# Routing for the first expert taken apart: records in a tensor of their own, one-hot products 128 columns wide, other experts' tables and the last scatters behind the branch

## The chip, the cores and the metric

One core of one Trainium2 chip runs the whole program. The metric is device time in microseconds, from launch to the end of the last engine; the median of three runs of the kernel before is 544.47 us (544.14 to 545.3). Engines are named as in the profile: PE multiplies matrices (PEld loads its weights), DVE, ACT and POOL work on 128 partitions at a time, SP issues loads and stores.

## What is computed

B = 1, S = 2048 tokens, D = 512, F = 1792, E = 8 experts, float32. Layer A is a long causal convolution, gated, with a residual; layer B sends each token to the one expert with the highest logit.

```python
h = x + q_ln * y                 # y: short conv of k, times v, long conv over S, plus kv * ssm_D
xf = layernorm(h)
logits = xf @ w_gate
topk_idx = argsort(-logits)[:, :1]
gates = softmax(topk_val)        # one value: 1
for e in range(E):
    mask = topk_idx == e
    out += (gates * mask) * (silu(xf @ w1[e]) @ w2[e])
h2 = h + out
```

## The kernel before

The program has three stages, all with an order written out by hand for each engine (a manual schedule: an engine runs its instructions in program order and waits on semaphores).

**Convolution and logits (0 to 182 us).** A planner interleaves loads, transposes, products with Toeplitz windows and DVE and POOL work. At its end, for each 128-wide block c of D, `logits(c, p)` (L388) multiplies the transposed rows with the gate weights; `sum_logits` adds the result to `lacc`. `h_dram` holds one row of 516 numbers per token: 512 of h, then mean, 1/std, gate and a spare.

**Routing (182 to 198.6 us).** PE transposes `lacc` into `pl` (L618). DVE finds each token's expert as a one-hot `oh` (P x E x NJ: token p of column j, NJ = 16), and a scan `incl` of it along j. PE makes the counts of the experts (`pn`) and the rank of every token within its expert (`pr`, L644, L645). DVE then makes `key` (count and index, L652), the sorted order of the experts (`gt`, `sr`, `eqm`, `perm_i`), and each token's place `c_i` in a table of 8 experts x 4 tiles x 128 rows, of which 24 tiles are kept. The place splits into a tile `col_i` and a row `lo_f`. `ohhi` marks the tile, POOL multiplies it with the token's number (`vt`), and `ohlo` marks the row; sixteen products `ohlo` x `vt` (L687), one for each j, add up to the table `ptab` (128 rows x 24 tiles) of token numbers plus one. From it come `idxg` (rows to gather) and, on POOL, `idxs` and `half_i` (rows to scatter to, with a large number for empty places). Two gathers on POOL (L707) fetch the first two tiles of the first expert (the smallest one); SP loads its first two weight chunks `raw` (L715). `keep_warm` (L605) issues products that nobody reads.

**Branch and experts (198.6 us to the end).** `over`, `nover` and `wide_i` compare the sizes of the experts with a list of capacities; every engine loads `wide_i` and jumps (L948). This input takes the block `experts(SNUG)`, laid out right behind. In it the experts run smallest first of `ORDER`: `norm` and `turn_x` normalise and transpose the gathered rows (`xr`, then `xh` and `xl`, a high and a low part), ACT and DVE split each weight chunk into `whi` and `wlo`, `up` (L821) makes acc = three sets of products, ACT its silu `s`, DVE `hh`, POOL `hl`; `down` (L842, L845) goes back; `send` (L855 and L857) adds the residual into `o` and scatters `o` to `out_dram` on POOL. In an expert's `up`, from chunk 3 on, POOL issues the gathers of the next expert's rows (`hr`, L759), one each chunk. The last expert's last rows leave in two halves. Behind the block stands the program's end (L1119): a DRAIN on each engine, SP's walk over all semaphores, and a barrier.

Of the kernel before, what the change touches and what calls it, by code (L numbers as in the profile page):

```python
# [11 lines left out]
I32 = mybir.dt.int32  # L12
AF = mybir.ActivationFunctionType
# [11 lines left out]
RW = D + 4  # L25
# [106 lines left out]
def kernel(  # L132
# [8 lines left out]
    h_dram = dram.tile([S, RW], F32, name="h_dram")  # L141
# [23 lines left out]
    iota_b = keep.tile([P, P], F16, name="iota_b")  # L165
# [11 lines left out]

    conv = ExitStack()
# [253 lines left out]
    def casts():  # L432
# [3 lines left out]
        for a, n in ((iota_b, "iota"), (tri_b, "tri"), (one_b, "one"), (tile_b, "tile")):  # L436
            nc.gpsimd.tensor_copy(a, const(n))
# [5 lines left out]
    nc.gpsimd.memset(wgc, 0.0)  # L443
    nc.scalar.activation(mv1[:, 0, 0:1], lacc[:, 0:1], AF.Copy)
# [155 lines left out]

    conv.close()
# [3 lines left out]
    def keep_warm(n, width):  # L605
        for _ in range(n):
# [3 lines left out]
    bc = lambda a, n: a.unsqueeze(2).to_broadcast([P, NJ, n])  # L610
# [8 lines left out]
    keep_warm(5, 128)  # L619
# [7 lines left out]
    nc.vector.reciprocal(rec[:, :, 1], rec[:, :, 1])  # L627
# [16 lines left out]
    nc.tensor.matmul(pr, tri_b, oh, start=True, stop=False)  # L644
    nc.tensor.matmul(pr, one_b, incl, start=False, stop=True)  # L645
# [6 lines left out]
    nc.vector.scalar_tensor_tensor(key, pn, float(E), const("key"), op0=ALU.mult, op1=ALU.add)  # L652
# [3 lines left out]
    gt = small([E, E], "gt")  # L656
    nc.vector.tensor_tensor(gt, key.unsqueeze(1).to_broadcast([P, E, E]),
                            key.unsqueeze(2).to_broadcast([P, E, E]), op=ALU.is_gt)
    sr = small([E], "sr")
    nc.vector.tensor_reduce(sr, gt, axis=AX.X, op=ALU.add)  # L660
    eqm = small([E, E], "eqm", parts=1)
    eqe = small([E, E], "eqe", parts=1)
    nc.vector.tensor_tensor(eqm, sr[0:1].unsqueeze(1).to_broadcast([1, E, E]),
                            const("si")[0:1].rearrange("p (i e) -> p i e", e=E), op=ALU.is_equal)
    nc.gpsimd.tensor_tensor(eqe, eqm, const("ei")[0:1].rearrange("p (i e) -> p i e", e=E), op=ALU.mult)

    r2 = small([E, NJ], "r2")
    nc.vector.scalar_tensor_tensor(r2, sr.unsqueeze(2).to_broadcast([P, E, NJ]), 4096.0, pr,
                                   op0=ALU.mult, op1=ALU.add)
    nc.vector.tensor_tensor(r2, r2, oh, op=ALU.mult)  # L670
    with nc.allow_low_precision(reason="whole numbers under 8"):
        nc.vector.tensor_reduce(perm_i, eqe, axis=AX.X, op=ALU.add)
    with nc.allow_low_precision(reason="whole numbers under 32768"):
        nc.vector.tensor_reduce(c_i, by_j(r2), axis=AX.X, op=ALU.add)
    nc.vector.tensor_scalar(col_i, c_i, 7, None, op0=ALU.logical_shift_right)
    nc.vector.scalar_tensor_tensor(lo_f, col_i, -float(P), c_i, op0=ALU.mult, op1=ALU.add)

    ohhi = small([NJ, 24], "ohhi", F16)
    nc.vector.tensor_tensor(ohhi, tile_b.unsqueeze(1).to_broadcast([P, NJ, 24]), bc(col_i, 24),
                            op=ALU.is_equal)  # L680
    vt = small([NJ, 24], "vt", F16)
    nc.gpsimd.tensor_tensor(vt, ohhi, bc(tok_b, 24), op=ALU.mult)
    ohlo = ohlo_f.bitcast(F16).rearrange("p (j m) -> p j m", j=NJ)
    ptab = ps_t.tile([P, 24], F32, name="pt")
    for j in range(NJ):
        nc.vector.tensor_scalar(ohlo[:, j, :], iota_b, lo_f[:, j:j + 1], None, op0=ALU.is_equal)
        nc.tensor.matmul(ptab, ohlo[:, j, :], vt[:, j], start=j == 0, stop=j == NJ - 1)  # L687
    keep_warm(4, 432)
# [5 lines left out]
    nc.vector.tensor_scalar(idxg, ptab, -1.0, 0.0, op0=ALU.add, op1=ALU.max)  # L694
# [3 lines left out]
    tabs = small([24], "tabs")  # L698
    nc.scalar.activation(tabs, ptab, AF.Copy)


    first = ctx.enter_context(tc.tile_pool(name="first", bufs=1))
    rows0 = []
    for t in range(2):
        hr = first.tile([P, RW], F32, name=f"first{t}")
        col = 3 * ORDER[0] + t
        nc.gpsimd.indirect_dma_start(  # L707
            out=hr, out_offset=None, in_=h_dram[:, :],
            in_offset=bass.IndirectOffsetOnAxis(ap=idxg[:, col:col + 1], axis=0))
        rows0.append(hr)  # L710
# [19 lines left out]
    def experts(caps):  # L730
# [392 lines left out]
```

## Time and profile before

The profile is of one execution on the chip.

| | |
|---|---|
| median of 3 runs | 544.47 us |
| the profiled execution, its time | 544.39 us |
| its span, first to last instruction | 542.5 us |
| mean granted clock of PE | 0.991 |
| PE busy | 519.1 us (96%) |
| DVE busy | 405.6 us (75%) |
| ACT busy | 265.1 us (49%) |
| POOL busy | 260.7 us (48%) |

Groups and timeline rows read: start or busy time, engine, line, operation, tile written and tiles read (buffer numbers left out), sizes, count, and in brackets how long the engine had been idle and what ended that. Rows of one source line read: engine, operation, count, least, median and greatest duration in ns, and the start of the first and of the last. PE and its weight loads PEld are listed apart.

### The profile page before, as it was taken

How to read it: one execution, taken by the hardware profiler on the slowest of the kernel's cores; microseconds unless marked ns; L12 is line 12 of the kernel's file. 1: busy time of each engine (PE TensorE's matmuls, PEld its weight loads, DVE VectorE, ACT ScalarE, POOL GpSimd, SP SyncE). 2: the span in 40 equal slices, each digit the busy share in tenths (PEclk: the TensorE clock that was granted, in tenths of full speed). 3: DMA queues.
4: the chain of work that ended last, by engine and by line, in shares of the span. 5: the costliest groups of instructions: out<-in, count | busy, mean ns of one | idle time of the engine just before them, and what ended most of it. 6: DMA issues, size and time to landing. Idle time of an engine off the chain costs nothing. (4 is left out here: it accounts for less than half of the span.)

```text
span 542.5 us, 12152 instructions
## 1 busy us (share of the span) xinstructions
PE 519.1 (96%) x4812; PEld 451.9 (83%) x4812; DVE 405.6 (75%) x558; ACT 265.1 (49%) x410; POOL 260.7 (48%) x297
## 2 busy tenths in 40 slices
PE   9999989999998699999999999999999999999994
PEld 9867767767656469789999999999988988988973
DVE  3779899898997968859855784974884784785851
ACT  2697887544320346545435445545543644554520
POOL 0555659865641136618503921840760760851832
PEclk9999999999999989999999999999999999999998
DMA  8918786659661278674654665674676566576401
GB/s 285 380 55 261 236 276 195 179 153 287 187 170 43 60 263 320 218 256 166 199 182 140 204 199 166 189 259 141 206 219 233 180 210 231 194 219 205 155 2 41
DMA packets 42468, 105.26 MB, mean 194 GB/s; under 512 B 6480, under 2 KB 14800, under 8 KB 42018
## 3 DMA queue, kind: packets, MB, share of 16 engines
q1 hardware_dynamic: 39602, 95.89, 54.9%
q0 software_dynamic: 2800, 8.51, 4.9%
q8 instruction: 40, 0.66, 0.5%
q14 instruction: 26, 0.21, 0.1%
HBM read 95.96 MB, written 8.47 MB: 193 GB/s over the span
## 5 line engine op out<-in xcount | busy, mean ns | idle before, releaser
L826 POOL TENSOR_TENSOR hl<-s,hh 128x240 fp32r<-128x240 f32 (+5 forms) x112 | 114.4, 1035 | 162.2 <-DVE hh L825 161.7
L807 DVE TENSOR_TENSOR wlo<-raw,whi 128x1024 fp32r<-128x1024 f32 x112 | 160.5, 1443 | 38.8 <-ACT whi L806 35.2
L806 ACT ACTIVATE whi<-raw 128x1024 fp32r<-128x1024 f32 x112 | 114.6, 1051 | 3.5 <-DMA raw<-in_w_dram 3.5
L824 ACT ACTIVATE s<-acc 128x240 f32<-128x240 f32 (+5 forms) x112 | 43.1, 387 | 98.1 <-PE acc L821 63.4
L825 DVE CAST hh<-s 128x240 fp32r<-128x240 f32 (+5 forms) x112 | 55.0, 501 | 30.1 <-ACT s L824 29.9
L821 PE MATMUL acc<-xh,whi 128*128 128x240 f32 (+5 forms) x448 | 73.0, 285 | 0.1
L821 PE MATMUL acc<-xh,wlo 128*128 128x240 f32 (+5 forms) x448 | 72.0, 283 | 0.0
L821 PE MATMUL acc<-xl,whi 128*128 128x240 f32 (+5 forms) x448 | 71.9, 283 | 0.0
L821 PEld LDWEIGHTS acc<-xh,whi 128*128 128x128 f32 x448 | 61.7, 189 | 0.8 <-ACT xh L782 0.3
L821 PEld LDWEIGHTS acc<-xl,whi 128*128 128x128 f32 x448 | 61.6, 189 | 0.0
L821 PEld LDWEIGHTS acc<-xh,wlo 128*128 128x128 f32 x448 | 61.4, 189 | 0.0
L842 PE MATMUL acc<-whi,hh 128*128 128x512 f32 (+2 forms) x136 | 54.3, 399 | 0.0
L842 PE MATMUL acc<-whi,hl 128*128 128x512 f32 (+2 forms) x136 | 53.6, 394 | 0.0
L842 PE MATMUL acc<-wlo,hh 128*128 128x512 f32 (+2 forms) x136 | 53.5, 394 | 0.0
L265 POOL TENSOR_TENSOR acc<-acc,ac 128x512 f32<-128x512 f32 x26 | 33.1, 1280 | 37.1 <-ACT acc L253 19.2
L845 PE MATMUL acc<-hh,whi 128*128 128x304 f32 (+2 forms) x168 | 49.8, 296 | 0.0
L845 PE MATMUL acc<-hl,whi 128*128 128x304 f32 (+2 forms) x168 | 49.2, 293 | 0.0
L845 PE MATMUL acc<-hh,wlo 128*128 128x304 f32 (+2 forms) x168 | 49.1, 292 | 0.0
L296 ACT ACTIVATE st<-pa 128x512 f32<-128x512 f32 x64 | 37.3, 595 | 20.6 <-PE pa L293 20.3
L293 PEld LDWEIGHTS pa<-kv,tw 128*128 128x128 f32 x256 | 30.2, 191 | 12.2 <-ACT st L296 8.7
L293 PE MATMUL pa<-kv,tw 128*128 128x128 f32 x256 | 33.5, 282 | 2.2 <-ACT st L296 2.2
L782 ACT ACTIVATE xh<-pt 128x512 fp32r<-128x512 f32 (+5 forms) x18 | 9.6, 535 | 53.1 <-PE pt L781 53.1
(171 smaller groups left out, 878.2 us busy)
## 6 DMA issues: line engine op xcount, KB each, us to landing
raw<-in_w_dram SPq DMA_DIRECT2D x112, 512.0 KB
tv<-in_tab_v_dram SPq DMA_DIRECT2D x12, 512.0 KB
h<-in_q_dram SPq DMA_DIRECT2D x16, 256.0 KB
kt<-in_kt_dram SPq DMA_DIRECT2D x3, 1216.0 KB
v<-in_v_dram SPq DMA_DIRECT2D x12, 256.0 KB
kern<-in_ssm_dram SPq DMA_DIRECT2D x12, 256.0 KB
h<-in_x_dram SPq DMA_DIRECT2D x12, 256.0 KB
h_dram<-h SPq DMA_DIRECT2D x12, 256.0 KB
```

The lines of the kernel that those rows point to most:

```text
L265: nc.gpsimd.tensor_add(T[a, c, u], T[a, c, u], T[b, c, u])
L293: nc.tensor.matmul(p[:, :, j], tw[:, u * UJ + j, r, :], src[:, j, :], start=True, stop=True)
L296: nc.scalar.activation(T["s" + kind, c][:, r * NU + u], T["pa", kind, c, u, r], AF.Copy)
L782: nc.scalar.activation(xh[:, at, r0:r0 + m], pt[:, :, :m], AF.Copy)
L806: nc.scalar.activation(whi, raw, AF.Copy)
L807: nc.vector.tensor_sub(wlo, raw, whi.bitcast(F32))
L821: nc.tensor.matmul(pu, a[:, k, fs], b[:, k, :], start=i == 0, stop=i == 3 * ND - 1)
L824: nc.scalar.activation(s, pu, AF.Silu)
L825: nc.vector.tensor_copy(hh[:, f, :], s)
L826: nc.gpsimd.tensor_sub(hl[:, f, :], s, hh[:, f, :].bitcast(F32))
L842: nc.tensor.matmul(pd[:ds_.stop - ds_.start], b[:, f, ds_], a[:, f % 2, :], start=f == 0 and i == 0, stop=f == last - 1 and i == 2)
L845: nc.tensor.matmul(pd, a[:, f % 2, ds_], b[:, f, :], start=f == 0 and i == 0, stop=f == 2 * NCH - 1 and i == 2)
```

## The change

- **Records apart.** `h_dram` has 512 columns; mean, 1/std and gate go to `rec_dram` (S x 4). Each gather of rows becomes two: the row, then its record. For the first two tiles of the first expert the record is not gathered ahead of the work: mean and 1/std come from products (below), and the gate's record is gathered while that expert is in its down phase.
- **Only the first expert first.** `least` is the smallest `key`, its low three bits the expert's index; the first weight loads use it. Places `c_i` are counted by expert, not by rank in the order of sizes (PE adds 32 e through a product with `base_b`). Before the branch only the two marks `A_0` of the first expert's tiles are made. The marks of all 24 tiles, their products, `order_of_experts` and `other_tables` stand in the branch.
- **Tables in the kt buffer.** `iota_b`, `tile_b`, `base_b`, all marks and the first rows lie in the buffer of the Toeplitz windows, with j innermost; POOL writes the constants after the plan. `ohlo` is made by two operations (9 and 7 values of j) and also has j innermost, so that each product reads 128 columns that lie 16 elements apart, as weights and as moving operand.
- **Mean and 1/std by products.** `parts` splits both into three bf16 parts; POOL multiplies them with the marks; sixteen products `pv0` pick them, `mr0` sums the parts.
- **Unread products.** `stay_warm` 2, 3 and 5 in the last logits, `keep_warm` 8 and 8 for 5 and 5, 2 of 512 columns for 4 of 432, 3 before the last transposes.
- **First chunk.** `wlo` in two halves around `xr`; both columns of chunk 0 run together.
- **End.** The last three `o` have tiles of their own (`ends`), and their scatters stand behind the branch.

```diff
-    h_dram = dram.tile([S, RW], F32, name="h_dram")
+    h_dram = dram.tile([S, D], F32, name="h_dram")
+    rec_dram = dram.tile([S, 4], F32, name="rec_dram")
...
+        if c == ND - 1:
+            stay_warm((3, 5)[p])
...
+    least = small([1], "least", I32)
+        nc.vector.tensor_reduce(least, key, axis=AX.X, op=ALU.min)
+    nc.vector.tensor_scalar(least, least, E - 1, None, op0=ALU.bitwise_and)
...
-    for j in range(NJ):
-        nc.vector.tensor_scalar(ohlo[:, j, :], iota_b, lo_f[:, j:j + 1], None, op0=ALU.is_equal)
-        nc.tensor.matmul(ptab, ohlo[:, j, :], vt[:, j], start=j == 0, stop=j == NJ - 1)
-    keep_warm(4, 432)
+    def selected(to, at, dt, js=range(NJ)):
+        window = columns(at - P, P, dt)
+        for j in js:
+            nc.tensor.matmul(to, ohlo_f.bitcast(dt).rearrange("p (m j) -> p m j", j=NJ)[:, :, j], window[:, :, j], start=j == 0, stop=j == NJ - 1)
...
+    for js in (range(0, 9), range(9, NJ)):
+        at = slice(js[0], js[-1] + 1)
+        nc.vector.tensor_tensor(ohlo[:, :, at], iota_b[:, :, at],
+                                lo_i[:, at].unsqueeze(1).to_broadcast([P, P, len(js)]), op=ALU.is_equal)
+        selected(ptab0, A_V, F16, js)
+    pv0 = ps_t.tile([P, P], F32, name="pt")
+    selected(pv0, A_T, BF16)
+    keep_warm(2, 512)
...
+        marks(A_T, A_T, 24)
+        ptab = ps_u.tile([P, P], F32, name="acc")
+        selected(ptab, A_0, F16)
+        norm(0, *firsts[0])
...
+        order_of_experts()
+        other_tables()
...
-        store(E - 1, *first_rows)
+        store(E - 1, *first_rows, ends[0])
...
     with sizes.Else():
         experts(SNUG)
+    scatter(out, idxs[:, end - 1:end], ends[0], S)
+    for i in range(2):
+        scatter(halves, half_i[:, i:i + 1], ends[i + 1], 2 * S)
```

DVE, from `key` to the row marks `ohlo`, in the kernel before (its lines; `r` is `r2`, `pt` the rank in PSUM):

```order
L652 SCALAR_TENSOR_TENSOR key<-pn,cs 128x8
L657 TENSOR_TENSOR gt<-key 128x64
L660 TENSOR_REDUCE sr<-gt 128x8
L663 TENSOR_TENSOR eqm<-sr,cs 1x64
L668 SCALAR_TENSOR_TENSOR r_2402<-sr,pt 128x128
L670 TENSOR_TENSOR r_2402<-r_2402,oh 128x128
L672 TENSOR_REDUCE perm_i<-eqe 1x8
L674 TENSOR_REDUCE c_i<-r_2402 128x16
L675 TENSOR_SCALAR col_i<-c_i 128x16
L676 SCALAR_TENSOR_TENSOR lo_f<-col_i,c_i 128x16
L679 TENSOR_TENSOR ohhi<-tile_b,col_i 128x384
L686 TENSOR_SCALAR ohlo_f<-iota_b,lo_f 128x128 x16
```

The same stretch of DVE in the changed kernel (its lines; `kt` is the buffer that holds constants and marks):

```order
L679 SCALAR_TENSOR_TENSOR key<-pn,cs 128x8
L682 TENSOR_REDUCE least<-key 128x1
L683 TENSOR_SCALAR least<-least 128x1
L695 TENSOR_TENSOR r_2431<-pr,oh 128x128
L697 TENSOR_REDUCE c_i<-r_2431 128x16
L698 TENSOR_SCALAR col_i<-c_i 128x16
L699 TENSOR_SCALAR lo_i<-c_i 128x16
L703 TENSOR_TENSOR kt<-kt,col_i 128x32
L704 TENSOR_TENSOR kt<-kt,tok_b 128x32
L720 TENSOR_TENSOR ohlo_f<-kt,lo_i 128x128x9
L720 TENSOR_TENSOR ohlo_f<-kt,lo_i 128x128x7
```

The sorting of the experts and the 384-wide tile marks have left this place; `least` and two 32-wide marks have come, and sixteen row marks have become two.

PE around the branch, before (L687 the last of the sixteen products, L781 the transposes of the first and of the last rows, L821 the first expert products):

```order
L687 MATMUL pt<-vt,ohlo_f 128x24
L607 MATMUL warm<-cs 128x432 x4
L947 TENSOR_LOAD wide_i
L948 COMPARE_AND_BRANCH
L781 MATMUL pt<-cs,xr 128x128 x4
L781 MATMUL acc<-cs,xr 128x112 x4
L821 MATMUL acc<-xh,whi 128x240 x4
```

PE around the branch now (L709 the products, first the last of `pv0`, then the sixteen of `ptab`, of which the first is shown with its weight load; L853 the transposes, L983 products that nobody reads):

```order
L709 MATMUL pt<-kt,ohlo_f 128x128
L636 MATMUL warm<-cs 128x512 x2
L1035 TENSOR_LOAD wide_i
L1036 COMPARE_AND_BRANCH
L709 LDWEIGHTS ohlo_f
L709 MATMUL acc<-kt,ohlo_f 128x128
L853 MATMUL pt<-cs,xr 128x128 x4
L983 MATMUL acc<-cs 128x128 x3
L853 MATMUL acc<-cs,xr 128x112 x4
L898 MATMUL acc<-xh,whi 128x240 x8
```

Between the branch and the transposes now stand sixteen products that wait for DVE's marks, and three products between the first transposes and the last.

POOL at the end, before (`o` the rows to scatter, L948 the jump out of the block):

```order
L826 TENSOR_TENSOR hl<-s,hh 128x240 x2
L857 DMA out_dram<-o,idxs 2048x512
L826 TENSOR_TENSOR hl<-s,hh 128x240 x9
L857 DMA out_dram<-o,idxs 2048x512
L857 DMA out_dram<-o,half_i 4096x256 x2
L948 UNCONDITIONAL_BRANCH
```

POOL at the end now: first the end of the block, with the jump at L1036, then what stands behind the branch:

```order
L783 DMA out_dram<-o,idxs 2048x512
L903 TENSOR_TENSOR hl<-s,hh 128x240 x2
L783 DMA out_dram<-o,idxs 2048x512
L903 TENSOR_TENSOR hl<-s,hh 128x240 x9
L1036 UNCONDITIONAL_BRANCH
```

Behind the branch:

```order
L783 DMA out_dram<-end_2519,idxs 2048x512
L783 DMA out_dram<-end_2520,half_i 4096x256
L783 DMA out_dram<-end_2521,half_i 4096x256
L1217 UNCONDITIONAL_BRANCH
L1217 ISA
```

The three last scatters have moved behind the jump; each still waits for DVE's write of its rows.

More of the change, by code (lines that the diff above doesn't have):

```diff
@@ L164 @@
     idxs = keep.tile([P, 24], I32, name="idxs")
-    iota_b = keep.tile([P, P], F16, name="iota_b")
+    idx0 = keep.tile([P, 2], I32, name="idx0")
     tri_b = keep.tile([P, P], BF16, name="tri_b")
@@ L386, in gate_w, with stay_warm @@
         return wgc[:, a:a + NU * E]
+    def stay_warm(n):
+        if "late" not in T:
+            pt("pb", "late", [P, NG, 512])
+        for _ in range(n):
+            nc.tensor.matmul(T["late"][:, 0, :P], const("one"), cs[:, :P], start=True, stop=True)
     def logits(c, p):
@@ L435, in casts @@
             nc.gpsimd.tensor_scalar_add(rungs[:, 0, i], rungs[:, 1, i], 8.0 * (SNUG[i] - TIGHT[i]))
-        for a, n in ((iota_b, "iota"), (tri_b, "tri"), (one_b, "one"), (tile_b, "tile")):
+        for a, n in ((tri_b, "tri"), (one_b, "one")):
             nc.gpsimd.tensor_copy(a, const(n))
@@ L655 @@
     nc.scalar.activation(small([1], "unread"), mx[:, 0:1], AF.Silu)
[L656 to L665, printed above, removed]
-    r2 = small([E, NJ], "r2")
[L668 to L672, printed above, removed]
+    r2 = small([E, NJ], "r2")
+    nc.vector.tensor_tensor(r2, pr, oh, op=ALU.mult)
     with nc.allow_low_precision(reason="whole numbers under 32768"):
@@ L743, in experts @@
         LEAD, AHEAD = 4, 8
[L744 to L745 removed]
+        X = {("hr", 0, t): rows0[t] for t in range(2)}
+        W, RAW, PV = {}, {}, {}
         def tiles(n):
@@ L917, in experts @@
                 wlo = wlo.rearrange("p (k f) -> p k f", k=ND)
-                up(n, 2 * r, whi, wlo)
-                if n and r - 1 < len(tiles(n - 1)) and r:
-                    store(n - 1, *tiles(n - 1)[r - 1])
-                up(n, 2 * r + 1, whi, wlo)
+                for fs in ([0, 1],) if s == 0 else ([2 * r], [2 * r + 1]):
+                    up(n, fs, whi, wlo)
+                    if n and r - 1 < len(tiles(n - 1)) and r and not fs[0] % 2:
+                        store(n - 1, *tiles(n - 1)[r - 1])
                 if 3 <= r and n + 1 < E:
-                    gather(n + 1, r - 3)
+                    for i in range(2):
+                        gather(n + 1, 2 * (r - 3) + i)
             else:
@@ L977 @@
             colf = g1p.tile([P, NJ], F32, name="colf")
-            nc.vector.tensor_copy(colf, col_i)
+            step = g1p.tile([P, E], F32, name="step")
+            nc.vector.tensor_sub(step, sr, const("e"))
+            there = g1p.tile([P, E, NJ], F32, name="there")
+            nc.vector.tensor_tensor(there, oh, step.unsqueeze(2).to_broadcast([P, E, NJ]), op=ALU.mult)
+            nc.vector.tensor_reduce(colf, by_j(there), axis=AX.X, op=ALU.add)
+            nc.vector.tensor_scalar(colf, colf, 32.0, None, op0=ALU.mult)
+            nc.vector.tensor_add(colf, colf, col_i)
             lo = g1p.tile([P, NJ], F32, name="lo")
-            nc.vector.tensor_copy(lo, lo_f)
+            nc.vector.tensor_copy(lo, lo_i)
             for j in range(NJ):
```

277 lines of the change are left out of this document (171 added, 106 removed).

## The prediction

> **What bounds the kernel now.** I read first the table of busy times by stage, then the timeline of the routing stage, then what ran after the last scatter. The table gives, for each stretch, its length and the busy time (and count) of PE, PEld, DVE, ACT and POOL, then the granted clock, the DMA share and GB/s:
>
> ```profile
> 182.30:187.90 5.60, 3.31 (x24) 2.85 (x24) 5.11 (x23) 3.40 (x6) 1.19 (x5) 1.00 0.14 5
> 187.90:194.70 6.80, 5.67 (x21) 3.37 (x22) 4.26 (x23) 1.25 (x2) 2.99 (x3) 0.50 0.57 171
> 194.70:198.56 3.86, 2.84 (x12) 1.26 (x11) 3.02 (x10) 1.00 (x3) 2.44 (x6) 1.00 0.64 186
> 198.56:534.80 336.24, 336.24 (x2384) 315.18 (x2384) 239.58 (x280) 161.39 (x253) 156.54 (x148) 1.00 0.59 195
> ```
>
> From 198.56 to 534.80 PE is busy for all 336.24 us: there only an interruption of PE can cost, and nothing that merely relieves another engine can gain. Time can be had ahead of 198.56 and behind 534.80. Ahead of it, the path runs through DVE, PE and POOL in turn:
>
> ```profile
> 182.33 0.33 PE L618 MATMUL pl<-cs,lacc 128*128 128x128 f32 x1 [1.01 <-DVE lacc L399]
> 182.50 1.48 PE L607 MATMUL warm<-cs 128*128 128x128 f32 x10
> 185.33 0.17 DVE L652 SCALAR_TENSOR_TENSOR key<-pn,cs 128x8 f32<-128x8 f32 x1
> 187.42 0.17 DVE L676 SCALAR_TENSOR_TENSOR lo_f<-col_i,c_i 128x16 f32<-128x16 int32 x1
> 187.52 0.55 DVE L679 TENSOR_TENSOR ohhi<-tile_b,col_i 128x384 f16<-128x384 bf16 x1
> 187.99 3.32 DVE L686 TENSOR_SCALAR ohlo_f<-iota_b,lo_f 128x128 f16<-128x128 f16 x16
> 191.06 0.24 DVE L686 TENSOR_SCALAR ohlo_f<-iota_b,lo_f 128x128 f16<-128x128 f16 x1
> 189.03 2.53 PE L687 MATMUL pt<-vt,ohlo_f 128*128 128x24 f16 x16 [2.25 <-DVE ohlo_f L686]
> 191.73 0.16 DVE L694 TENSOR_SCALAR idxg<-pt 128x24 int32<-128x24 f32 x1
> 192.04 0.16 DVE L697 TENSOR_REDUCE wide_i<-nover 1x2 int32<-1x16 f32 x1
> 192.20 1.20 POOL L707 DMA_INDIRECT first<-h_dram,idxg  x1 [3.22 <-DVE wide_i L697]
> 193.71 0.95 POOL L707 DMA_INDIRECT first<-h_dram,idxg  x1 [0.30 <-issue]
> 196.51 0.63 PE L781 MATMUL pt<-cs,xr 128*128 128x128 f32 x4 [0.33 <-DVE raw L797]
> 197.24 0.74 DVE L772 TENSOR_SCALAR xr<-first 112x256 f32<-112x256 f32 x2 [0.84 <-DMA first<-h_dram,idxg]
> 197.71 0.74 PE L781 MATMUL acc<-cs,xr 112*128 112x112 f32 x4 [0.57 <-DVE xr L772]
> 198.56 0.38 PE L821 MATMUL acc<-xh,whi 128*128 128x240 f32 x1
> ```
>
> The 16 one-hot masks set the pace of the 16 products, the products give idxg at 191.89, the first gather starts 0.31 later, the second at 193.71, its rows are used 3.53 after its start, and the first product of the experts follows 1.32 after that. So from idxg's end to the first expert product lie 198.56 - 191.89 = 6.67 us, all of it the two gathers and what follows them.
>
> Behind the last product:
>
> ```profile
> 534.34 0.96 POOL L857 DMA_INDIRECT out_dram<-o,half_i  x1 [0.30 <-issue]
> 535.61 0.95 POOL L857 DMA_INDIRECT out_dram<-o,half_i  x1 [0.30 <-POOLq L948]
> L948 POOLq COMPARE_BRANCH  x1: 46/46/46, 535.4 to 535.4; - x1
> L1119 POOLq DRAIN  x3: 46/102/3311, 538.3 to 542.2; - x3
> L1119 SPq EVENT_SEMAPHORE  x12: 17/28/28, 539.8 to 542.4; - x12
> L1119 SPq DRAIN  x3: 7/7/13, 540.4 to 541.9; - x3
> L1119 POOLq EVENT_SEMAPHORE  x4: 17/17/17, 541.7 to 542.4; - x4
> L1119 DVEq DRAIN  x2: 10/34/58, 538.0 to 541.9; - x2
> ```
>
> The last scatter ends at 536.56. POOL has taken the end-of-branch jump at 535.4, but its next instruction, a DRAIN, starts only at 538.3: 1.76 us after the scatter. That DRAIN takes 3.31, to 541.6, and at 541.7 POOL opens the closing barrier. SP is through its own walk of semaphores (the last half's landing seen at 539.8) by 540.4 to 540.5. So POOL ends last, by about 1.15 us over SP.
>
> **The change, part by part.** All sums are against the profiled execution (544.39 us, span 542.5), 0.08 below the median of 544.47, which I leave out.
>
> *Start of routing.* Five unread fp32 products now stand between the last logits and pl. Ten rows of L607 are five products in 1.48 us; less the tail of the last, 0.27 each. PE was idle 1.01 there. The logits end near 181.4 and are held up perhaps 0.1 by the two earlier products; five take 1.35, so pl starts near 182.85: **+0.5** (bounds 0 and +0.7). L627's reciprocal leaves the place ahead of cand: **-0.17**, the length of its like (L676). From key (185.33) to the masks (187.99) stood 2.66 us:
>
> ```profile
> 185.53 0.23 DVE L657 TENSOR_TENSOR gt<-key 128x64 f32<-128x64 f32 x1
> 186.83 0.35 DVE L674 TENSOR_REDUCE c_i<-r 128x16 int32<-128x128 f32 x1
> 187.22 0.17 DVE L675 TENSOR_SCALAR col_i<-c_i 128x16 int32<-128x16 int32 x1
> ```
>
> gt, sr, eqm, perm_i, the scaling in r2 and the 384-wide ohhi go, while least (two small operations) and two 32-wide marks come. That leaves key and eight operations ahead of the masks; a small one starts 0.2 after the one before (key to gt, col_i to lo_f), c_i holds 0.39 and r2 0.3, so I count 2.1: **-0.56**. Masks start at 187.99 + 0.5 - 0.17 - 0.56 = 187.76.
>
> *Masks.* 16 operations become two, of 1152 and 896 elements. L686 takes 0.24 for 128 f16 elements and the 16-element L676 0.17, so 0.61 ns an element and 0.16 fixed: 0.86 + 0.71 = 1.57. By the other row, ohhi's 0.55 for 384 mixed elements, it is 1.03 ns: 1.36 + 1.10 = 2.46. I take 1.57, as types and comparison are L686's, and keep 2.46 as a bound.
>
> The Trainium skill ("VectorE: DVE Perf Modes", the perf-mode tier table) gives a tensor_tensor two elements a cycle when all tensors are 16-bit with step 1; by it the pair would take some 1.4 us, an estimate, and the sum would be 0.2 better.
>
> *Products.* This term decides. Three sets of 16 (indices, mean and rstd, the other tables) now read 128 columns 32 bytes apart on both sides. No strided product is in the trace. The bounds are the contiguous bf16 ones and the fp32 ones:
>
> ```profile
> 185.15 0.22 PE L644 MATMUL pt<-oh,tri_b 128*128 128x128 bf16 x1
> 185.20 0.22 PE L645 MATMUL pt<-incl,one_b 128*128 128x128 bf16 x1
> 185.25 1.53 PE L607 MATMUL warm<-cs 128*128 128x128 f32 x10
> ```
>
> Starts 0.05 apart for bf16; for fp32 some 0.13 a row at most (1.53 less the last 0.28, by nine), 0.118 in the four transposes of L781 (0.63 less 0.27, by three). I take p = 0.085, between, as the format is the first row's and one column at a time the second's. The first product starts at 187.76 + 0.86 + 0.06 = 188.68; PE is then the slower of the two engines, and idx0 is ready 16p + 0.42 later (L687's 0.2, a semaphore, L694's 0.16): 190.46, against 191.89. The gathers keep their 6.67, so **by the gathers** the first expert product comes at 195.77 + 16p = 197.13.
>
> *The path beside it* is new, and PE is on it. 32 products end at 188.68 + 32p; mean and rstd are ready 0.6 later; DVE then loads wide_i and branches (0.85: wide_i ended at 192.20, the branch below stood at 192.8, and I add 0.25 for its first instruction), makes the marks of 24 columns (two 384-wide operations, 0.9), which 16 more products wait for (16p). Then PE has the transposes of the first rows (0.5), three unread products (0.8), the last transposes and the way to the first product (197.71 to 198.56, 0.85).
>
> ```profile
> L948 DVEq COMPARE_BRANCH  x1: 55/55/55, 192.8 to 192.8; - x1
> ```
>
> **By PE**: 188.68 + 0.6 + 0.85 + 0.9 + 0.5 + 0.8 + 0.85 + 48p = 193.18 + 48p = 197.26. Later than the gathers by 0.1, so routing gains 198.56 - 197.26 = **1.3 us**. Bounds: p = 0.05 gives 196.8 (gain 1.7, masks and gathers binding); p = 0.118 gives 198.84 (loss 0.3); slow masks hold the seven late products back 0.84, gain 0.5.
>
> Against p speaks a rule. The Trainium skill ("SBUF — State Buffer", the note on cachelines) says that an access that crosses to a new 16-byte line pays a penalty, free strides ending at 8 bf16 elements; here the step is 16. It gives no price for PE; a doubled p of 0.17 would make 201.3, a loss of 2.8. The skill's "TensorE: Matmul & The Clock Gate" (Weight-path perf modes) allows the fast weight load for 128 columns "packed or strided", which speaks for p near 0.085. No row here decides.
>
> *Weights.* The first two raw loads hang on least instead of perm_i and come earlier; rec's store moves behind them on SP and is first read when expert 0 is in its down phase or later. Cost 0; covered by some 30 us.
>
> *Experts.* 19 gathers of records join POOL's queue, with hl's of the next columns behind each:
>
> ```profile
> L759 POOL DMA_INDIRECT hr<-h_dram,idxg x17 | 20.2, 1189 | 2.8 <-issue 2.2
>   ACT s L824: 33.2, 29
> ```
>
> At hr's 1.19 plus 0.2 that is 26.4 us, POOL going from 156.5 to 183 of 336. ACT already waits for hl (the second row, 33.2 us in 29 waits) while PE stays full, thanks to six accumulators and eight weight buffers. I take 0; if a tenth came through it would be 2.6. On DVE the order of experts and tables (eight small operations, some 2 us) now stand ahead of wlo of chunk 2; DVE idled around those, waiting for whi:
>
> ```profile
> 199.82 2.46 DVE L807 TENSOR_TENSOR wlo<-raw,whi 128x1024 fp32r<-128x1024 f32 x2 [0.56 <-ACT whi L806]
> 203.06 1.23 DVE L807 TENSOR_TENSOR wlo<-raw,whi 128x1024 fp32r<-128x1024 f32 x1 [0.77 <-ACT whi L806]
> ```
>
> so 0, at worst 0.5.
>
> *Tail.* POOL leaves the branch after its last hl, about 8 us before the end, and the three scatters come after the jump. The last scatter is still released by o (535.3), but the DRAIN can start at 536.56: with its 3.31 kept, 539.87. Next late is SP at 540.48, which waits for the landing. Gain 541.63 - 540.48 = **1.1 us**. Bounds: 0, if the DRAIN really waits for the landing (539.8) and adds 1.8; 1.8, if the landing also comes sooner, as there is less code traffic beside it.
>
> The skill's "Runtime: NRT & Kernel Launch" (Instruction fetch mechanics) says that a taken branch outside the window of two pages stalls for a fetch; the 2.9 us from 535.4 to 538.3 agree.
>
> Sum: 544.39 - 1.3 - 1.1 = **542.0**.
>
> **Rivals.** One more row for the first of them, POOL's next operation behind the second gather:
>
> ```profile
> 194.74 1.33 POOL L719 TENSOR_SCALAR emp<-tabs 128x24 f32<-128x24 f32 x1
> ```
>
> 1. *The tail gives nothing*, the DRAIN following the landing: 544.39 - 1.3 = 543.1. For it: nothing shows what the 3.31 are. Against: POOL ran emp behind its second gather, long before that gather's rows had landed, so an indirect DMA in flight doesn't hold the engine itself.
> 2. *Products at the fp32 pace, or slow masks*: 544.39 + 0.3 - 1.1 = 543.6, or 542.8. For it: fp32 rows are the only ones here that load column by column.
> 3. *Strided products slow* (the side of slower): at p = 0.2 the first expert product comes at 193.18 + 9.6 = 202.8, 4.2 late, total 547.5. It decides from p = (198.56 + 1.1 - 193.18)/48 = 0.135 on, and shows as slower from 0.16. The same happens at p = 0.17 if the clock halves as at 187.90 to 194.70 (0.50): 546.1. Against the clock: PE's fillers go from 5 to 8 products ahead of the masks, and the idle 2.25 us before L687 shrink to about 1.
> 4. *Record gathers reach PE*: 542.0 + 2.6 = 544.6.
>
> **How the numbers follow.** Forecast 0.50, rivals in order 0.18, 0.15, 0.11, 0.06. About 0.2% (1.1 us) is what a measurement here can tell. Faster takes the forecast, 0.14 of rival 1 and 0.05 of rival 2: 0.69. Slower is rival 3 and a little of 4: 0.13. The rest, 0.18, is the same. The range goes from both gains at their best (1.7 + 1.8: 540.9) to products at the fp32 pace without a gain in the tail (544.7).
>
> **What would show it.** idx0's end near 190.5; the start-to-start of the strided products (0.085); the first expert product near 197.3, and whether DVE's xr or PE's tables came last before it; a granted clock of 1.00 through the routing; PE full from there to its last product, in the same 336 us; POOL's DRAIN right behind the last scatter, and its length. A pitch over 0.13, or a DRAIN that still ends 6 us after the last scatter's start, proves the forecast wrong.

## The result, and the profile after

| | before | after |
|---|---|---|
| median, same chip | 544.36 us (4 runs, 544.14 to 545.3) | 550.43 us (4 runs, 549.91 to 552.4) |
| ratio | | 1.0115, 95% interval 1.0087 to 1.0142 |
| profiled execution | 544.39 us, span 542.5 | 550.5 us, span 548.6 |
| first expert product | 198.56 us | 205.07 us |
| last scatter starts | 535.61 us | 541.93 us |

The kernel became 6.1 us slower, where a gain of 2.4 (to 542.0) had been forecast; it lies outside the range. The profiled executions differ by 6.1 too, so they can be compared step by step. The busy table by stage of the kernel after, same columns as before:

```profile
187.90:194.70 6.80, 6.38 (x27) 4.00 (x28) 2.47 (x9) 2.01 (x3) 2.28 (x3) 0.69 0.46 160
194.70:198.56 3.86, 3.86 (x11) 1.89 (x9) 1.76 (x6) 1.05 (x2) 1.16 (x3) 0.50 0.50 138
198.56:202.00 3.44, 3.44 (x14) 1.78 (x13) 1.71 (x8) 0.00 (x0) 0.00 (x0) 0.68 0.54 151
202.00:534.80 332.80, 332.55 (x2366) 311.76 (x2365) 224.69 (x285) 160.83 (x255) 172.07 (x171) 1.00 0.60 196
```

PE, which had been idle for 1 us in each of the first two stretches, is all but full in them now, while DVE does less (2.47 for 4.26 us): PE has become what the routing waits for. The timeline of the kernel after in the routing, PE first, then DVE's and POOL's rows:

```profile
182.64 0.33 PE L646 MATMUL pl<-cs,lacc 128*128 128x128 f32 x1
188.32 7.81 PE L709 MATMUL pt<-kt,ohlo_f 128*128 128x128 f16 x32 [0.63 <-DVE ohlo_f L720]
195.95 3.60 PE L636 MATMUL warm<-cs 128*128 128x512 f32 x4
199.34 3.99 PE L709 MATMUL acc<-kt,ohlo_f 128*128 128x128 f16 x16
203.14 0.62 PE L853 MATMUL pt<-cs,xr 128*128 128x128 f32 x4
205.07 1.19 PE L898 MATMUL acc<-xh,whi 128*128 128x240 f32 x8 [0.26 <-ACT xh L854]
187.30 1.86 DVE L720 TENSOR_TENSOR ohlo_f<-kt,lo_i 128x1152 f16<-128x1152 int16 x2
192.37 0.16 DVE L731 TENSOR_SCALAR idx<-pt 128x2 int32<-128x2 f32 x1 [2.70 <-PE pt L709]
196.17 0.17 DVE L739 TENSOR_REDUCE mr<-pt 128x4 f32<-128x12 f32 x1 [2.99 <-PE pt L709]
197.50 0.36 DVE L704 TENSOR_TENSOR kt<-kt,tok_b 128x384 f16<-128x384 f16 x1
197.77 0.54 DVE L844 TENSOR_SCALAR xr<-kt,mr 128x512 f32<-128x512 f32 x1
192.83 1.20 POOL L760 DMA_INDIRECT kt<-h_dram,idx  x1 [4.22 <-DVE wide_i L734]
```

The group of these products (busy time, mean ns of one, idle time before) gives the length of one:

```profile
L709 PE MATMUL pt<-kt,ohlo_f 128*128 128x128 f16 (+1 forms) x32 | 7.8, 419 | 0.6 <-DVE ohlo_f L720 0.6
```

The 32 strided products take 7.81 us, so from start to start (7.81 less the last one's 0.42, by 31) 0.238 us; the 16 of the other tables take 3.99, the same pace. DVE waits for them twice, 2.70 us ahead of the indices and 2.99 ahead of mean and rstd. The rows themselves do not wait any more: xr of the first tile stands at 197.77, ready ahead of the products of the other tables, which the transposes of L853 are queued behind. The marks that these products read are ready at 197.86 (L704); but until 199.34 PE is at the two unread fp32 products of 512 columns (L636, four rows of the profile), which stand ahead of them in its order; a row takes 0.85 us at a granted clock of 0.50.

And the end, the last scatter of the timeline, and then the rows of the closing line:

```profile
541.93 0.97 POOL L783 DMA_INDIRECT out_dram<-end,half_i  x1 [0.31 <-DVE end L934]
```

```profile
L1217 POOLq EVENT_SEMAPHORE  x4: 17/17/17, 547.8 to 548.5; - x4
L1217 POOLq DRAIN  x3: 46/112/6056, 541.7 to 548.3; - x3
```

The DRAIN stands at 541.7, right at the last scatter, but lasts 6.056 instead of 3.311. It ends at 547.8, 5.8 us after the last scatter's start; before it was 541.6 - 535.61 = 6.0.

### The profile page after: what moved, and what is told of

It reads as the page before. It is cut to its first block, busy times and chain, and to the rows that moved or that the text cites. A ratio compares the mean times of both kernels' runs of the same rounds, so it can differ in the third digit from the quotient of the medians.

```text
span 548.6 us, 12335 instructions
## 1 busy us (share of the span) xinstructions
PE 530.8 (97%) x4879; PEld 460.4 (84%) x4879; DVE 391.1 (71%) x556; ACT 264.1 (48%) x410; POOL 279.3 (51%) x324
## 4 chain that ended last, share of the span: by engine, by line
PE 85%; DVE 5%; issue 4%; ACT 3%; DMA 1%; POOL 1%; POOLq 0%; DVEq 0%
PE acc L898 29%; PE acc L919 15%; PE acc L922 12%; PE pa L295 8%; PE pb L331 7%; PE pa L367 5%; PE pa L459 2%; PE pm L279 2%; DMA kt<-in_kt_dram 1%; PE pt L709 1%; PE pt L853 1%; DVE xa L344 1%; DVE zs L352 1%; PE pt L942 1%; ACT ac L263 1%
## 5 line engine op out<-in xcount | busy, mean ns | idle before, releaser
L880 DVE TENSOR_TENSOR wlo<-raw,whi 128x1024 fp32r<-128x1024 f32 (+1 forms) x113 | 154.0, 1374 | 35.7 <-ACT whi L875 35.6
L903 POOL TENSOR_TENSOR hl<-s,hh 128x240 fp32r<-128x240 f32 (+5 forms) x112 | 103.1, 938 | 134.3 <-DVE hh L902 133.8
L902 DVE CAST hh<-s 128x240 fp32r<-128x240 f32 (+5 forms) x112 | 47.9, 435 | 54.6 <-ACT s L901 54.4
L922 PEld LDWEIGHTS acc<-hh,whi 128*128 128x128 f32 x168 | 31.6, 188 | 0.1
```

The costliest lines, as they stand in the source:

```text
L880: nc.vector.tensor_sub(wlo[:, a:b], RAW[s][:, a:b], whi[:, a:b].bitcast(F32))
L902: nc.vector.tensor_copy(hh[:, f, :], s)
L903: nc.gpsimd.tensor_sub(hl[:, f, :], s, hh[:, f, :].bitcast(F32))
L922: nc.tensor.matmul(pd, a[:, f % 2, ds_], b[:, f, :], start=f == 0 and i == 0, stop=f == 2 * NCH - 1 and i == 2)
```

## The experiments

Thirteen kernels ran. The medians are of 10 to 12 runs each, against 17 to 23 of the kernel before on the same chip, except e2 (4 runs) and e4, e5, e6 (one run with a profile).

| run | from | time, us | before, us | ratio, 95% interval | first expert product |
|---|---|---|---|---|---|
| e1_narrow | after | 544.2 | 544.14 | 0.9996, 0.9985 to 1.0008 | 197.01 |
| e2_weights | after | 556.93 | 544.14 | 1.0237, 1.0219 to 1.0254 | 210.56 |
| e3_groups | after | 544.9 | 544.14 | 1.0018, 1.0008 to 1.0029 | 198.52 |
| e4_tail | before | 545.64 | 544.14 | one run | 199.69 |
| e5_pairs | after | 544.01 | 544.39 | one run | 197.43 |
| e6_single | after | 555.38 | 544.39 | one run | 209.50 |
| e7_groups_narrow | e3 | 543.65 | 544.39 | 0.9992, 0.9978 to 1.0005 | 196.61 |
| e8_no_late | e7 | 543.9 | 544.39 | 0.9986, 0.9969 to 1.0002 | 196.53 |
| e9_no_records | e7 | 543.38 | 544.17 | 0.9987, 0.9973 to 1.0002 | 197.12 |
| e10_more_s | e7 | 543.98 | 544.17 | 0.9993, 0.9978 to 1.0008 | 198.27 |
| e11_bridge | e10 | 545.08 | 544.03 | 1.0017, 0.9992 to 1.0043 | 197.67 |
| e12_two_bridges | e11 | 543.44 | 544.03 | 0.998, 0.9965 to 0.9996 | 197.38 |
| e13_sooner | e12 | 542.66 | 544.33 | 0.9973, 0.9961 to 0.9985 | 196.57 |

**Which side of the product is slow?** e1 keeps every address and step of both operands and multiplies only the 2, 12 or 24 columns that are read later:

```diff
-        window = columns(at - P, P, dt)
+        window = columns(at - n, n, dt)
...
-            nc.tensor.matmul(to, ohlo_f.bitcast(dt)...
+            nc.tensor.matmul(to[:, P - n:], ohlo_f.bitcast(dt)...
...
-        selected(ptab0, A_V, F16, js)
+        selected(ptab0, A_V, F16, 2, js)
...
```

> The changed kernel, with each of the 48 products moving only the columns that are read (2, 12 and 24 instead of 128); both sides still lie 32 bytes apart. In the changed kernel these products start 0.238 us apart. Theory A, the strided moving side sets that pace: start to start falls to about 0.10, 48 x 0.138 = 6.6 us less on the path through PE, the first expert product near 198.5 and the time near 544. Theory B, the strided weight side sets it: start to start stays over 0.2 and the time near 550. Rival C, PE's granted clock sets it (0.50 for most of the stage): the pace was the same 0.24 at a clock of 1.00 (188 to 190 us) and at 0.50 (193 to 196), so C expects no fall here unless the clock comes back.

e2 makes the other side contiguous: `ohlo` (the weights) has m innermost, the moving columns stay 32 bytes apart.

```diff
-    ohlo = ohlo_f.bitcast(F16).rearrange("p (m j) -> p m j", j=NJ)
+    ohlo = ohlo_f.bitcast(F16).rearrange("p (j m) -> p m j", j=NJ)
...
```

> The changed kernel, with the row marks written so that the 128 weights of a product lie side by side; the moving side is still 128 columns 32 bytes apart. Theory A (moving side): start to start stays at about 0.24, the time near 550; the weight loads fall from 0.146 to 0.10 us without effect. Theory B (weight side): start to start falls to about 0.1, the time near 544. DVE's two mask operations write with a step of 256 bytes now and may take longer than 0.96 and 1.04.

The products of e1 in four of its rows (the last of the three sets is `acc<-kt`), then those of e2 with the masks ahead of them:

```profile
189.50 1.61 PE L709 MATMUL pt<-kt,ohlo_f 128*128 128x2 f16 x23 [0.19 <-DVE ohlo_f L720]
190.97 1.96 PE L636 MATMUL warm<-cs 128*128 128x512 f32 x4
193.00 1.17 PE L709 MATMUL acc<-kt,ohlo_f 128*128 128x24 f16 x16
197.01 1.20 PE L898 MATMUL acc<-xh,whi 128*128 128x240 f32 x8 [0.18 <-ACT xh L854]
```

```profile
186.86 9.27 DVE L720 TENSOR_TENSOR ohlo_f<-kt,lo_i 128x1152 f16<-128x1152 int16 x2
196.18 5.50 PE L709 MATMUL pt<-kt,ohlo_f 128*128 128x128 f16 x23 [1.73 <-DVE ohlo_f L720]
204.90 3.91 PE L709 MATMUL acc<-kt,ohlo_f 128*128 128x128 f16 x16
```

With two moving columns and weights still 32 bytes apart the pitch falls to about 0.064 (1.61 less the last one's 0.2, by 22). With contiguous weights and 128 strided moving columns it stays at 0.23 (3.91 less 0.42, by 15). So the moving side sets it, and the weights' step adds at most 0.005. e1's median falls from 550.43 to 544.2: the whole loss against the kernel before lies in these products, and with them cured the forecast gain is still not there. e2's total says nothing on the products: its masks are now written in steps of 256 bytes and take 9.27 us for 1.86.

**What does a step cost?** e3 keeps 128 columns and lays `ohlo` and the table out in four groups of four j (steps of 8 bytes); e5 does it in eight groups of two (4 bytes), e6 with sixteen of one (contiguous). The core of e3; e5 and e6 differ in G:

```diff
-        return place_f.bitcast(dt)[...].rearrange("p (c j) -> p c j", j=NJ)
+        return place_f.bitcast(dt)[...].rearrange("p (g c j) -> p c g j", g=G, j=NJ // G)[:, at:at + n]
...
-    for js in (range(0, 9), range(9, NJ)):
+    for g in range(G):
...
```

> The changed kernel with all marks and constants laid out in four groups of four values of j, so that columns lie 8 bytes apart instead of 32 on both sides, 128 columns wide as before; row marks in four operations of 512 elements. Theory A with lines of 16 bytes (an access that crosses to a new line pays, two in a line do not): start to start falls to 0.06 to 0.12, and with it the first expert product to 198 to 199, the time to 543.5 to 545. Rival, any step over one element pays the same: 0.24 and 550. In between (0.12 to 0.16) would say that the cost goes by bytes.

> As the groups of four, but eight groups of two: columns 4 bytes apart on both sides, 128 wide. Found so far: 0.238 us from start to start at 32 bytes, 0.12 at 8 bytes, 0.05 at 2 bytes. If a line of 16 bytes costs a fixed time and its hits share it, down to one column a step (0.05 to 0.06), 4 hits a line give 0.06. If the cost goes by the bytes passed over, 0.08 to 0.09.

> Sixteen groups of one: both sides contiguous, 128 wide, as the products of the ranks are. Both theories: 0.05 to 0.065 from start to start once the masks are there. The masks are sixteen operations again, so the masks set the pace of the first sixteen products (0.16 to 0.2), and the gain shows in the two later sets.

The sixteen products of the other tables in e3, e5 and e6, a fence each:

```profile
194.73 2.04 PE L720 MATMUL acc<-kt,ohlo_f 128*128 128x128 f16 x16
```

```profile
193.61 1.13 PE L720 MATMUL acc<-kt,ohlo_f 128*128 128x128 f16 x16 [0.70 <-DVE kt L715]
```

```profile
168.99 10.10 POOL L639 CAST kt<-cs 128x2048 int16<-128x2048 f32 x1
172.28 6.68 DVE L374 TENSOR_TENSOR st<-st 128x512 f32<-128x512 f32 x1
206.69 1.06 PE L720 MATMUL acc<-kt,ohlo_f 128*128 128x128 f16 x16 [3.30 <-DVE kt L715]
```

Less the last one's 0.2 to 0.3 and divided by 15, the pitch is 0.12 at 8 bytes, 0.06 at 4 and 0.056 contiguous. From 8 to 32 bytes it doubles once more, to 0.238. e6's total is spoilt for other reasons. POOL writes the constants of the table as single elements 352 bytes apart, in 10.10 us; in e5 the same cast, in pairs, takes 1.95. DVE's operation beside it takes 6.68 us (0.69 in its next instance), and the convolution ends some 9 us late (pl at 191.44). In the routing DVE's two operations that mark all 24 tiles, laid out in the same way, take 1.98 and 1.97 us (0.50 and 0.49 in e5). None of this has to do with the products.

**The tail by itself.** e4 is the kernel before with the last three scatters moved behind the branch; their rows get tiles of their own, two of which POOL first fills with zeros:

```diff
+            if not late:
+                scatter(out, at, o, S)
...
+    scatter(out, idxs[:, end - 1:end], ends[0], S)
+    for i in range(2):
+        scatter(halves, half_i[:, i:i + 1], ends[i + 1], 2 * S)
```

> The kernel before with the last three scatters behind the branch and nothing else. In the kernel before POOL's last DRAIN ended 6.03 us after the last scatter's start, in the changed one 5.79, though there it began 2.9 us earlier against that scatter. Theory D, the DRAIN ends with the scatter's own work whatever its start: again 5.8 to 6.1, time 544.1 to 544.4. My prediction's theory, a DRAIN of 3.3 us: 4.3, time 543.3.

Its last scatter, and its closing line:

```profile
536.74 0.98 POOL L734 DMA_INDIRECT out_dram<-end,half_i  x1 [0.30 <-DVE end L868]
```

```profile
L1130 POOLq EVENT_SEMAPHORE  x4: 17/17/17, 542.9 to 543.6; - x4
L1130 POOLq DRAIN  x3: 46/108/6370, 536.5 to 543.4; - x3
```

The DRAIN starts at 536.5, lasts 6.37 and ends 6.1 us after the last scatter's start. (Its experts began 1.1 us later in that execution: 0.7 of it stands ahead of the routing, with pl at 183.03, and most of the rest in DVE's xr beside POOL's filling, 1.06 us for 0.74. So I compare only behind the scatter.) In the other profiles with the scatters behind the branch the distance is 5.8 to 6.7, the longest in e2. The DRAIN does not last a fixed time from its own start; it ends some 6 us after the last scatter begins.

**How much is left with fast products?** e7 joins e1 and e3: four groups, and only the columns that are read. e8 is e7 without the ten unread products of `stay_warm`.

> Groups of four and only the columns that are read. Theory A: products at 0.05 to 0.07, masks in four operations of 0.4, so idx0 near 189.2 against 190.3 with narrow products alone, the first expert product near 195.9 (before 198.56), PE off the path, time 542 to 543. If the time does not follow the first expert product, what was gained ahead of the experts is lost in them, and the wait stands in PE's rows there.

> The same without the ten unread products in the last logits. Theory: pl starts 0.5 to 0.7 earlier and all behind it, first expert product near 195.3, time 0.6 below the run with them. Rival: without them the granted clock falls in the routing, as in the kernel before (0.50 from 187.9), and the strided or narrow products and the transposes take longer, so that the gain is lost; the clock by windows shows it.

e7's first expert product stands at 196.61, 1.95 us earlier than before, but its median gains only 0.7 us, within its interval. (The profiled execution, 542.87, is among the fastest of the ten, which go from 542.8 to 545.4. What the slower ones lose is in no profile.) Its timeline near 225, PE, DVE and POOL, and behind it the longest row of its waits from 212 to 230 (us in total, times, longest):

```profile
225.96 0.66 PE L864 MATMUL pt<-cs,xr 128*128 128x128 f32 x4 [0.47 <-DVE xr L855]
219.11 0.37 DVE L913 CAST hh<-s 128x240 fp32r<-128x240 f32 x1 [2.00 <-ACT s L912]
223.28 0.38 DVE L913 CAST hh<-s 128x240 fp32r<-128x240 f32 x1 [1.80 <-ACT s L912]
225.36 0.54 DVE L855 TENSOR_SCALAR xr<-hr,rec 128x512 f32<-128x512 f32 x1
219.49 0.97 POOL L842 DMA_INDIRECT hr<-h_dram,idxg  x1 [0.16 <-issue]
220.76 1.35 POOL L842 DMA_INDIRECT rec<-rec_dram,idxg  x1 [0.30 <-issue]
222.13 1.37 POOL L914 TENSOR_TENSOR hl<-s,hh 128x240 fp32r<-128x240 f32 x2
```

```profile
ACT s L912 <- POOL hl L914: 6.7, 5, 2.9
```

Read from POOL on: a gather of rows and one of records stand on POOL ahead of each pair of `hl`; ACT waits up to 2.9 us for the `s` that `hl` frees (the second fence); DVE's casts wait for ACT; xr of expert 1 comes at 225.36, and PE's transposes, due when the products before them ended (225.09 + 0.40), start at 225.96. It is the only place in the experts where PE stands; e1's profile has the same gap (0.46 at 226.35).

e8 starts everything 0.5 us sooner (pl 182.04, indices 189.30), yet its first expert product stands at 196.53, and the eight products there take 1.98 us instead of 1.20, since the clock is 0.72 to 0.50 at 194 to 198: most of what the earlier start gave, the clock took.

**Is it the records?** e9 leaves the seventeen record gathers of experts 1 to 7 out; e10 keeps them and breaks the chain at ACT:

```diff
-                s = xp.tile([P, cap], F32, name="s", bufs=3)
+                s = xp.tile([P, cap], F32, name="s", bufs=5)
```

> e7_groups_narrow without the seventeen record gathers of experts 1 to 7: these experts use the first expert's mean, rstd and scale, so the output is not the reference's; everything else is issued as in e7. Theory R (each record gather holds POOL for about 1.3 us ahead of two hl, ACT waits for the s that hl frees, the whi behind it and DVE's wlo and xr come late, and PE stands still at the transposes of expert 1's first rows): PE is full from its first expert product on, xr of expert 1 stands ahead of its transposes, and the median falls by about 0.9 us against e7, to 542.7. Rival Q (the stall is due to the tables of the other experts on DVE, or to weights that arrive no earlier than before while PE starts 2 us earlier): the gap of some 0.9 us near 225 stays, and the median stays within 0.3 of e7's 543.65.

> e7_groups_narrow with five buffers for s (the activated rows that hh and hl are made from) in place of three, and nothing else changed; the record gathers stay. Theory R: ACT no longer waits 2.86 and 2.58 us for POOL's hl beside the record gathers of expert 1, whi and wlo come in time, the gap near 225 is gone or under 0.3, and the median falls to about 542.8. Rival Q: the gap stays at about 0.9 and the median within 0.3 of 543.65.

The stretch near expert 1 and xr of its first tile, in e9 and then in e10:

```profile
200.00:230.00 30.00, 29.90 (x208) 26.69 (x208) 27.78 (x36) 18.11 (x30) 24.63 (x25) 1.00 0.80 280
225.06 0.92 DVE L859 TENSOR_SCALAR xr<-hr,mr 128x512 f32<-128x512 f32 x1
```

```profile
200.00:230.00 30.00, 30.00 (x214) 27.36 (x213) 25.09 (x37) 17.76 (x29) 25.54 (x26) 1.00 0.82 285
223.24 0.55 DVE L855 TENSOR_SCALAR xr<-hr,rec 128x512 f32<-128x512 f32 x1 [0.69 <-DMA rec<-rec_dram,idxg]
```

Both profiles have PE full or all but full near expert 1 (29.90 and 30.00 us busy from 200 to 230, 29.53 in e7), without a wait of PE there. That alone shows little: in e8, with the records and with three buffers, PE is full there too (30.00), because its first products came late. The place of xr tells more. From the end of the indices to that xr it takes 35.5 us in e7 and 35.7 in e8, but 34.9 in e9 (225.06 - 190.21) and 32.9 in e10 (223.24 - 190.31). So theory R holds for the gap, by both of its links, though leaving the records out moves xr by 0.7 us only and breaking the chain at ACT by 2.6. It fails for the median, which moved by 0.3, down in e9 and up in e10, and not by 0.9 (the intervals of the three ratios overlap): in these two profiles the first expert product was 0.5 and 1.7 us later than in e7, e10's at a clock of 0.50 from 192 to 198.

**The clock.** e11 and e12 are e10 with more unread products, ahead of the masks and then also behind the tables' products:

```diff
-    keep_warm(8, 128)
+    keep_warm(10, 128)
...
         selected(ptab, A_0, F16, 24)
+        hold = ps_u.tile([P, P], F32, name="acc")
+        for _ in range(3):
+            nc.tensor.matmul(hold, const("one"), cs[:, :P], start=True, stop=True)
```

> e10_more_s with ten unread fp32 products in place of eight ahead of the masks, so that PE does not stand still near 188.3 before the first one-hot product. Theory C1 (the clock falls to 0.50 near 190.5 because PE stood still for about 0.6 us near 188.3): the granted clock stays at 1.00 from 187.9 to 194, the first expert product comes near 196.5 as in e7 or before, and the median falls to about 543.0. Rival C2 (the clock falls near 190.5 whatever PE did at 188): clock 0.50 for some 2 to 8 us as in e10, first expert product at 196.6 to 197.5, median within 0.4 of e10's 543.98.

> e11_bridge with three more unread products right behind the products of the other experts' table, so that PE is not idle near 194 to 195 either while it waits for the first rows. Theory C1: clock 1.00 throughout, first expert product near 196.5, median about 543.0, some 1.1 below before (ratio 0.998). Rival C2: the clock falls again, and the time is that of e11 within 0.3.

The table by stretches of two microseconds, columns as above, of e12:

```profile
187.90:190.00 2.10, 1.64 (x28) 1.40 (x28) 1.48 (x6) 1.36 (x2) 0.56 (x2) 1.00 0.60 168
190.00:192.00 2.00, 2.00 (x17) 1.00 (x15) 1.33 (x9) 0.56 (x1) 1.24 (x2) 0.62 0.94 365
192.00:194.00 2.00, 2.00 (x10) 0.76 (x9) 0.43 (x2) 1.46 (x2) 1.49 (x3) 0.52 0.66 157
194.00:196.00 2.00, 2.00 (x29) 2.00 (x27) 1.18 (x6) 0.31 (x1) 0.00 (x0) 1.00 0.37 125
```

The clock falls near 190 although PE's pause at 188 is shorter (0.38 us here, 0.45 in e11, 0.71 in e7), and in e1 and e5 it stayed at 1.00 from 187.9 to 194.7 with pauses of 0.63 and 0.59. So C1 fails. C2 holds for the fall, but not for its times: e11's median is 1.1 above e10's, e12's 1.6 below e11's. What makes the clock fall stays open; it is back at 1.00 by 194 here and in e11. e11's median is the worst of these, and its profile shows another stop, 1.69 us on PE at 234.65, for expert 1's third record:

```profile
226.76 1.82 POOL L842 DMA_INDIRECT rec<-rec_dram,idxg  x1 [0.30 <-issue]
232.23 0.54 DVE L855 TENSOR_SCALAR xr<-hr,rec 48x512 f32<-48x512 f32 x1 [4.40 <-DMA rec<-rec_dram,idxg]
234.65 0.41 PE L864 MATMUL pt<-cs,xr 48*128 48x48 f32 x4 [1.69 <-DVE xl L866]
```

The record lands 3.6 us after POOL is done with it, DVE stands 4.40 us and PE pays. e12's profile shows no such stop. So with five buffers the records reach PE in a second way, by their landing. e13 issues the gathers for expert 1 one chunk earlier:

```diff
-                if 3 <= r and n + 1 < E:
+                lead = 3 if n else 2
+                if lead <= r and n + 1 < E:
                     for i in range(2):
-                        gather(n + 1, 2 * (r - 3) + i)
+                        gather(n + 1, 2 * (r - lead) + i)
```

> e12_two_bridges with the gathers of expert 1's rows and records issued one chunk (some 4 us) earlier in expert 0; those of the later experts stay. Theory R2 (what is left of the early routing is lost, now and then, where DVE's xr of expert 1 waits for a record that lands late, 1.69 us in e11's profile, none in e12's): PE is full from the first expert product on in the profile, xr no longer waits for a record, the spread of the twelve runs falls below e12's 2.9 us, and the median falls by 0.3 to 0.8, to about 542.9. Rival R3 (expert 1's records cost e12 nothing; its spread comes from the granted clock around 190 to 200 and from the late records of other experts): median within 0.3 of e12's 543.44, spread as before.

Its timeline, and its table by stretches:

```profile
196.57 1.33 PE L909 MATMUL acc<-xh,whi 128*128 128x240 f32 x8
222.30 1.35 POOL L842 DMA_INDIRECT rec<-rec_dram,idxg  x1 [0.30 <-DMA kt<-h_dram,idx]
228.97 0.53 DVE L855 TENSOR_SCALAR xr<-hr,rec 48x512 f32<-48x512 f32 x1
```

```profile
200.00:230.00 30.00, 30.00 (x208) 27.03 (x207) 26.48 (x34) 17.93 (x30) 26.38 (x28) 1.00 0.77 270
230.00:526.00 296.00, 296.00 (x2110) 278.86 (x2109) 209.66 (x244) 141.36 (x221) 155.41 (x143) 1.00 0.57 190
```

The third record is issued 4.5 us earlier than in e11, xr waits for none, PE is full from 200 to 526, and the median is 542.66: 1.7 us below the kernel before (0.9973, interval 0.9961 to 0.9985) and 7.8 below the kernel after. Against e12, taken in another comparison, it is 0.8 lower; its spread went from 2.9 us (542.02 to 544.87) to 2.3 (542.37 to 544.7). That is as R2 has it, on a small margin: the two ratios' intervals overlap. The profiles do not show that the earlier gathers made the difference: PE waits in neither, and e13's first expert product came 0.81 us sooner than e12's, 0.54 of it ahead of the routing (pl at 182.36 for 182.90). So e13 beats the kernel before and the kernel after, but its lead over e12 is not shown to be the gathers'.

## Why the prediction was wrong, point by point

The step that failed is the price of a strided product, which the prediction called the term that decides. It took p = 0.085 between a contiguous 0.05 and fp32's 0.118 and gave 0.11 to p near 0.2. The measured p is 0.238, outside both ends: neither row was a bound for it, since neither read a strided operand.

- **Products.** By the prediction's own sum the first expert product comes at 193.18 + 48 x 0.238 = 204.6; it came at 205.07. The path by PE decides, as the sum has it, and rival 3 is what happened, from its point of decision (0.135) on and beyond its price (0.2). The last 0.47 is a balance. The first product started 0.36 sooner than summed, DVE's steps up to the marks took 0.33 less, the transposes and what follows 0.22 less. Against these stand some 1.4 us for a term that the sum doesn't have, the unread products ahead of the last sixteen (see the clock, below). The rule that the prediction quoted against itself, the Trainium skill ("SBUF — State Buffer", the note on cachelines), had the right sign, and the estimate made with it (p = 0.17) was nearer than mine; e3 and e5 show how its threshold has to be read (below).
- **Start of routing and masks.** pl 0.31 late (forecast 0.5), partly by luck: the unread products hold it 0.68 us behind the last `lacc`, which was 0.06 before, but the convolution ended 0.31 sooner in this execution. Masks begin at 187.30 for 187.76 and take 1.86 for 1.57, within the bounds. The first product stands at 188.32 for 188.68. Together this was better than forecast by a third of a microsecond.
- **Indices.** 192.53 (192.37 + 0.16) for 190.46. With narrow columns the same steps give 190.30 (e1) and 189.83 (e7). The gain that the forecast saw was there, and the products took it.
- **The gathers' path.** 6.67 us from the indices to the first expert product were kept as a constant. Measured in e1 and e7: 197.01 - 190.30 = 6.71 and 196.61 - 189.83 = 6.78. Held there, but not everywhere: in e8 to e13 it is 6.9 to 8.0, the longest in e10, whose clock was 0.50 from 192 to 198.
- **Clock.** I argued that more fillers keep it up. It fell to 0.50 from 192 to 200, with PE busy throughout. The strided products did not care: their pitch is 0.238 ahead of the fall and in it. The unread fp32 rows did: the sum has no term for them, and at 0.85 us each they held PE until 199.34, while the marks stood at 197.86. In e1, at a clock of 1.00, the same four rows took 0.43 each, and the products started right behind the marks (193.00 for 192.89). So the wrong argument cost some 1.4 us, which the smaller differences named under the products hide in the sum.
- **Experts at 0.** Held for the kernel after: from the first expert product to the last scatter 336.86 us, 337.05 before, so the record gathers cost it nothing that shows. Once the routing is early PE does stand for 0.5 us in e7 and for 1.7 in e11, where xr comes too late for it; rival 4 is a rival of the repaired kernel.
- **Tail 1.1.** 0.2 measured (548.6 - 541.93 = 6.67 behind the last scatter's start, 6.89 before). The row "3311" was read as a duration that the DRAIN always takes; it was what was left of some 6 us that began with the scatter. Rival 1 was right. Its own reason (following the landing) has support but is not shown: in twelve of the fifteen profiles the DRAIN ends 2.8 to 3.0 us after the last packet on POOL's DMA queue, whether that packet comes 2.8 or 3.8 us behind the scatter's start or between; in the kernel before, e4 and e9 it is 2.1 to 2.3.

Together: + 6.51 up to the first expert product, - 0.19 from there to the last scatter, - 0.22 in the tail make 6.1, which is the whole difference.

## What to carry to other kernels

When a matmul's moving operand is cut out of a table, lay it out so that the columns of one product lie next to each other, or move only the columns that will be read; 128 columns 32 bytes apart cost four times as much as contiguous ones. Two rows of a trace bound an operation only if they differ from it in nothing that may matter: a step, a type and a width are three things, not one. Unread products that stand ahead of wanted ones are a term of the path, to be priced at the lower clock as well. And before a duration is kept as a constant, ask what it is counted from: here the last DRAIN's end followed the last scatter's start, and starting the DRAIN sooner gave next to nothing (0.2 us).

## What the runs showed of the hardware

- **Pitch of a 128-column 16-bit product by the step of its moving columns:** 0.056 us at 2 bytes, 0.06 at 4, 0.12 at 8, 0.238 at 32. The last is 1.86 ns a column; half of that at 8 bytes, where two columns share 16 bytes, fits one fixed price for each 16 bytes touched, hidden at four columns per line but not at two. The Trainium skill ("SBUF — State Buffer", the note on cachelines) has two hits per line as enough; for this operand two still cost double, and four were needed. That the line is the cause is argued from these four points, not shown by itself; below 32 bytes both operands' steps were changed together.
- **That pitch does not depend on the granted clock** (in the kernel after, sixteen products at 0.50 from 192.15 take 3.98 us and eight at 1.00 from 201.24 take 2.08: 0.237 each), and a PE that shows as busy from 190 to 200 was granted 0.50 from 192 on all the same.
- **Writing single 16-bit elements far apart is dear, and for the neighbour too.** In e2 DVE's masks in steps of 256 bytes took 9.27 us for 1.86, and POOL's products beside them 5.16 for 1.29. In e6 POOL's cast in steps of 352 bytes took 10.10, and a 512-element operation of DVE beside it 6.68 for 0.69. Short runs are enough to avoid it: the same cast took 1.95 in pairs (e5) and 1.88 in fours (e3).
- **POOL's last DRAIN** ended 5.8 to 6.7 us after the last scatter's start in the fifteen profiles, whether it began 0.2 to 0.3 us ahead of that scatter or 2.7 behind.
